# Spread products of the scales moved ahead of a slot's down products

## The chip, the cores and the metric

One core of one Trainium2 chip. The metric is the device time of one execution in microseconds (us), the median of the runs. TensorE multiplies (PE in rows; PEld is its loading of weights), VectorE is DVE, ScalarE is ACT, GpSimd is POOL, SyncE (SP) issues the transfers.

## The reference

Local and strided attention over 4 sequences of 576 tokens, 8 heads of 64, then two feed-forward layers over the 2304 tokens, all in float32:

```python
def _moe_ref(x, w_in, w_out) -> np.ndarray:
    h = x @ w_in
    g = h * np.cos(h)
    return (g @ w_out).astype(np.float32)
...
def _moe2_ref(x, w_gate, w_val, w_out) -> np.ndarray:
    g = x @ w_gate
    silu = g * (1.0 / (1.0 + np.exp(-g)))
    val = x @ w_val
    return (silu * val @ w_out).astype(np.float32)
```

The first layer is 512 to 2048 to 512 wide, the second 512 to 1536 to 512.

## The kernel before, in words

Every float32 factor is multiplied as two float16 parts, high and low, in three matmuls (`mm3`, L541 to L543). Before it is split, a matrix is multiplied by a power of two, its scale, so that its largest value fits. There are ten such scales for blocks of tokens and five for weights (w_in, w_out, w_gate, w_val, w_out2).

How a scale is made: VectorE takes the largest value per partition, column by column (L174 or L227 for weights, L521 for tokens). `spread_tops` takes the largest of the columns (L120), keeps its exponent (L123, L125 or L128) and multiplies an identity with it (L130): a diagonal of 128 values, `tops`. `common_scale` multiplies a matrix of ones with that diagonal on TensorE (L136, the spread product, 128x128 into a PSUM bank), so that all partitions hold all values, reads the largest (L137, `q`), and makes the scale and its inverse from it (L112 to L114).

The program is written out in the order of its engines. The tokens are in five blocks of 512, 512, 512, 384 and 384. In the first layer a slot is one block and one of 16 column tiles of w_in: `up1` is twelve matmuls (four contraction tiles times three) into a bank; `up1_a` to `up1_e` make the cosine product of them on ScalarE (L574, L581, L588), VectorE (L577, L584) and GpSimd (L589), spread over the next three slots; `up1_d` (L584) is the last to read the bank. `down_next` then multiplies the result of an older slot with w_out: twelve matmuls into four accumulators `acc0` to `acc3`, stored by L555 and L557 at a block's end. In the first HEAD = 14 slots there are no down products, and every second slot takes an accumulator's bank in place of one of its own (`spare`).

The main loop writes a slot in this order: the up products, the down products, `up1_a`, `up1_b` (L577), `finish`, one urgent piece (`pump_urgent`: splitting and scaling of the next block), half of the fill (`pump`: conversion and splitting of weights, their scans and scales), `up1_c`, `up1_d` (L584), the other half. A scale's steps are pieces of the fill or urgent pieces: one step makes the diagonal, a later one calls `common_scale`, which issues the spread product on TensorE behind all that the slot has there and reads it at once.

PSUM: four banks in a pool (`pm`), which the up products, the spread products and the products of the second layer take by turns through `bank()`; a tile takes the bank that was given free longest ago. The other four serve as accumulators.

Of the kernel before, what the change touches and what calls it, by code (L numbers as in the profile page):

```python
# [10 lines left out]
F32 = mybir.dt.float32  # L11
# [4 lines left out]
ALU = mybir.AluOpType  # L16
AX = mybir.AxisListType
# [14 lines left out]
LW = 64 + STRIDE  # L32
# [47 lines left out]
def build(tc, qk_l, qk_s, v_l, v_s, w_in, w_out, w_gate, w_val, w_out2, mask_l, mask_s, eye32, eye16, out):  # L80
    nc = tc.nc
    wide = w_in.dtype != F32
    with ExitStack() as ctx:
# [13 lines left out]
        ones16 = small.tile([128, 128], BF16, name="ones16")  # L97
# [5 lines left out]
        def col(name):  # L103
            count[0] += 1
            return small.tile([128, 1], F32, name=f"{name}{count[0]}")

        def brief(name):
            return small.tile([128, 1], F32, name=name, bufs=2)

        def finish_scale(p, bound):  # L110
            s, inv = col("s"), col("inv")
            nc.vector.reciprocal(out=s, in_=p)  # L112
            nc.vector.tensor_scalar(out=inv, in0=p, scalar1=2 / bound, scalar2=None, op0=ALU.mult)
            nc.vector.tensor_scalar(out=s, in0=s, scalar1=bound / 2, scalar2=None, op0=ALU.mult)  # L114
            return s, inv

        def spread_tops(parts, words):

            m, p = brief("m"), brief("p")
            nc.vector.tensor_reduce(out=m, in_=parts, op=ALU.max, axis=AX.X)  # L120
            if words:
                a = brief("a")
                nc.vector.tensor_scalar(out=a.bitcast(I32), in0=m.bitcast(I32), scalar1=3, scalar2=0x3F800000,  # L123
                                        op0=ALU.logical_shift_left, op1=ALU.bitwise_and)
                nc.vector.scalar_tensor_tensor(out=p.bitcast(I32), in0=m.bitcast(I32), scalar=0x40000000, in1=a.bitcast(I32),  # L125
                                               op0=ALU.bitwise_and, op1=ALU.bitwise_or)
            else:
                nc.vector.tensor_scalar(out=p.bitcast(I32), in0=m.bitcast(I32), scalar1=0x7F800000, scalar2=None, op0=ALU.bitwise_and)  # L128
            d = small.tile([128, 128], BF16, name="tops", bufs=2)
            nc.vector.tensor_scalar(out=d, in0=id16, scalar1=p, scalar2=None, op0=ALU.mult)  # L130
            return d

        def common_scale(d, bound):

            t, p = bank()[:, 0:128], brief("q")
            nc.tensor.matmul(out=t, lhsT=ones16, rhs=d, start=True, stop=True)  # L136
            nc.vector.tensor_reduce(out=p, in_=t, op=ALU.max, axis=AX.X)  # L137
            return finish_scale(p, bound)

        def prod(a, b, c=1.0, keep=True):  # L140
            r = col("c") if keep else brief("c")
# [6 lines left out]
        parts_w = {k: small.tile([128, a.shape[0] + 1], F32, name=f"pw_{k}") for k, a in MATS.items()}  # L148
# [30 lines left out]
        def later(cost, fn, key=None):  # L179
            fill.append((cost, fn, key))  # L180
# [3 lines left out]
        def step_fill():  # L184
            cost, fn, key = fill.popleft()
            fn()
            emitted.add(key)
            credit[0] -= cost

        def pump(share):  # L190

            credit[0] = min(credit[0] + share, max(share, 1.0))
            while fill and credit[0] > 0:
                step_fill()

        def need(key):
            while key not in emitted:
                step_fill()
# [53 lines left out]
        def begin(steps):  # L252

            if steps:
                later(*steps[0])
            while held:
                later(*held.popleft())
            held.extend(steps[1:])
# [24 lines left out]
        tops = {}  # L283

        def top_later(mat):
            begin([])
            later(0.6, lambda: tops.__setitem__(mat, spread_tops(parts_w[mat], wide)))

        def scale_later(mat, bound):
            later(0.6, lambda: scale_w.__setitem__(mat, common_scale(tops[mat], bound)))  # L290
# [81 lines left out]
        pm = ctx.enter_context(tc.tile_pool(name="pm", bufs=4, space=bass.MemoryType.PSUM))  # L372
# [26 lines left out]
        def load_v(i):  # L399
# [5 lines left out]
            else:  # L405
                v_t[i] = v_pair[i // 2 % 2]
                for u in range(2):
                    nc.sync.dma_start(out=v_t[i][64 * u:64 * u + SW, SP * u:SP * u + SP, :], in_=v_s[b, p % 2, u])

        def bank():  # L410
            return pm.tile([128, 512], F32, name="bank")

        def scale_q(i):
            q = qk_t[i][:, 0:S if is_local(units[i][1]) else QP]
# [100 lines left out]
        def scale_pieces(blk, scales):  # L515
            parts = small.tile([128, KC + 1], F32, name=f"parts{count[0]}_{blk}")
            count[0] += 1
            box = {}
            nc.gpsimd.memset(parts[:, KC:], TINY)
            for k in range(KC):  # L520
                yield 0.65, lambda k=k: nc.vector.tensor_reduce(out=parts[:, k:k + 1], in_=xy[blk][:, k, :], op=ALU.max, axis=AX.X,  # L521
                                                                apply_absolute_value=True)
            yield 0.6, lambda: box.__setitem__("top", spread_tops(parts, False))
            yield 0.6, lambda: scales.__setitem__(blk, common_scale(box["top"], TX))

        def split_pieces(blk, scales, dst):
            n = BLOCKS[blk][1]

            def piece(k):
                if k == 0:  # L530
                    dst[blk] = ring.tile([128, 2, 7, 512], F16, name="xs")
                t, s = dst[blk], scales[blk][0]
                if k < KC:
                    hi_part(t[:, 0, k, 0:n], xy[blk][:, k, :], s)
                if k:
                    lo_part(t[:, 1, k - 1, 0:n], xy[blk][:, k - 1, :], s, t[:, 0, k - 1, 0:n])
            for k in range(KC + 1):
                yield 0.7 if k else 0, lambda k=k: piece(k)
# [41 lines left out]
        def up1_c(c):  # L580
            nc.scalar.activation(out=c["w"], in_=c["w"], func=AF.Sin, scale=TWO_PI, bias=right)  # L581
# [188 lines left out]
        steps = deque()  # L770

        def keep_warm():
            t = bank()[:, 0:4 * LW].rearrange("p (n w) -> p n w", w=LW)
            nc.tensor.matmul(out=t, lhsT=id16, rhs=ml, start=True, stop=True)

        for k in range(len(gs) + LAGS[3] + 1):
            def group(lag):
                return gs[k - lag] if 0 <= k - lag < len(gs) else None
            i, g = 2 * (k // 6), k % 6
# [191 lines left out]
        def urge(pieces, key=None):  # L971
            urgent.extend((c, f, key) for c, f in pieces)
# [8 lines left out]
        def need_urgent(key):  # L981
            while key not in emitted or any(u[2] == key for u in urgent):
                pump_urgent()
# [24 lines left out]
        def load_w7(s):  # L1008
            if s < len(slots):
                need("pairs")  # L1010
                nc.sync.dma_start(out=w7_slots[s % W7S], in_=w7_d[slots[s][1]])

        for blk in range(NBLK):
            for m in range(M1):
                n = BLOCKS[blk][1]
                if slot < EARLY:
                    slot += 1
                    continue
                if blk == 0:
                    need(("in", m))  # L1020
                if m == 0:
                    if blk:
                        need_urgent(("xs", blk))
                    if blk == NBLK - 1:
                        urge(fold_pieces(0, sy, ys, spans), ("ys", 0))
                if m == (2 if blk else XM) and blk + 1 < NBLK:
                    urge(scale_pieces(blk + 1, sx))
                    urge(split_pieces(blk + 1, sx, xs), ("xs", blk + 1))
                c = up1(blk, m, spare=slot // 2 % KC if slot % 2 and slot < HEAD - 4 else None)
                if blk == NBLK - 1 and m in (7, 14):  # L1030
                    load_w7(m // 7 - 1)
                lag = 99 if slot < HEAD else max(MINLAG, HEAD - 2 - int((slot - HEAD) * RATE))
                work = 2.6 * n / 512
                while len(queue) + 1 > lag:
                    work += down_next()
                if slot >= HEAD:
                    open_weights(lag)
                up1_a(c)
                up1_b(steps[-1][2])
                if len(steps) > 2:  # L1040
                    finish(steps.popleft())
                budget = (work - 1.25 * n / 512) * (HSHARE if slot < HEAD else SHARE if blk < SB else SHARE2)
                pump_urgent()
                pump(budget * 0.5)
                up1_c(steps[-1][2])
                if len(steps) > 1:
                    up1_d(steps[-2][2])
                pump(budget * 0.5)
                steps.append((blk, m, c))
                slot += 1  # L1050
# [112 lines left out]
        for s, (blk, j) in enumerate(slots):  # L1163
            n = BLOCKS[blk][1]
            h = n // 2
            if s == 1:
                need(("out2", NPR - 1))
                for _ in range(RAW):
                    t = ring.tile([128, 512, 2] if wide else [128, 512], I32 if wide else F32, name="raw", bufs=RAW)
# [13 lines left out]
            w, x = w7_slots[s % W7S], ys[blk]  # L1183
# [139 lines left out]
```

## Time and profile before

| | |
|---|---|
| median of 3 runs | 900.7 us (898.19, 900.7, 902.98) |
| the profiled execution | 896.04 us, of which its span 894.3 |
| TensorE busy | 857.4 us, 96% |
| VectorE busy | 657.5 us, 74% |
| ScalarE busy | 521.7 us, 58% |
| mean granted TensorE clock | 0.984 |

A busy TensorE counts every matmul from its start to its end, and these overlap; its idle time is what is left. The attention ends at about 115 us, the first layer at about 515 us, the rest is the second layer. All fifteen spread products lie between 66 and 665 us.

### The profile page before, as it was taken

What the parts mean: (1) busy time and instruction counts of PE and PEld (TensorE: products, weight loads), DVE (VectorE), ACT (ScalarE), POOL (GpSimd) and SP (SyncE); (2) the same over time, 40 slices, a digit from 0 to 9 for tenths busy, and PEclk for the clock granted to TensorE, in tenths of its full rate; (3) what the DMA queues carried; (4) which work ended last, traced back from release to release, by engine and by line L of the source; (5) the groups of instructions that cost most, each with busy time, mean ns of one, the idle gap of its engine ahead of it and who ended that gap; (6) DMA issues with size and microseconds to landing.
All of it is one profiled execution on the core that took longest, in us unless ns stands there. A gap on an engine that the chain in (4) does not pass through costs nothing.

```text
span 894.3 us, 18463 instructions
## 1 busy us (share of the span) xinstructions
PE 857.4 (96%) x7228; PEld 607.3 (68%) x7228; DVE 657.5 (74%) x1287; ACT 521.7 (58%) x1046; POOL 198.7 (22%) x253
## 2 busy tenths in 40 slices
PE   7999999989999979899999998999999999999998
PEld 4677644434444434455655687888888899999998
DVE  4699899895758998969988368747765665665562
ACT  4789988763445668547888365545535434444440
POOL 3344324112134656422322200000000000000000
PEclk8699999999999989999999999999999999999999
DMA  9998842568545675661635435667777677888894
GB/s 293 345 319 252 268 150 68 166 191 270 195 142 192 214 234 184 220 208 49 218 124 207 165 142 199 261 207 262 245 235 270 223 264 283 308 284 320 310 331 155
DMA packets 53512, 200.61 MB, mean 224 GB/s; under 512 B 5456, under 2 KB 16208, under 8 KB 49584
## 3 DMA queue, kind: packets, MB, share of 16 engines
q1 hardware_dynamic: 53424, 199.42, 65.7%
q8 instruction: 57, 0.93, 0.4%
q14 instruction: 31, 0.25, 0.1%
HBM read 175.41 MB, written 23.99 MB: 223 GB/s over the span
## 4 chain that ended last, share of the span: by engine, by line
PE 73%; DVE 10%; ACT 6%; issue 6%; POOL 4%; DMA 1%; SPq 0%; ACTq 0%; POOLq 0%; DVEq 0%
PE acc L694 14%; PE bank L541 11%; PE bank L543 11%; PE bank L542 11%; PE acc L541 6%; PE acc L543 5%; PE acc L542 5%; PE bank L435 3%; PE po L488 3%; DVE arena L248 2%; POOL arena L916 2%; POOL arena L589 2%; ACT arena L245 2%; ACT arena L588 1%; PE tp L466 1%
## 5 line engine op out<-in xcount | busy, mean ns | idle before, releaser
L541 PE MATMUL bank<-xs,wi 128*128 128x256 f16 (+3 forms) x780 | 233.5, 299 | 20.3 <-DVE tb L584 9.9
L543 PE MATMUL bank<-xs,wi 128*128 128x256 f16 (+3 forms) x780 | 233.6, 300 | 0.0
L542 PE MATMUL bank<-xs,wi 128*128 128x256 f16 (+3 forms) x780 | 233.6, 299 | 0.0
L589 POOL TENSOR_TENSOR arena<-tb,arena 128x512 f16<-128x512 f32 (+1 forms) x80 | 91.6, 1146 | 241.7 <-ACT arena L588 219.0
L542 PEld LDWEIGHTS <-wi 128*128 128x128 f16 x880 | 86.2, 98 | 60.0 <-issue 27.6
L541 PE MATMUL acc<-arena 128*128 128x512 f16 (+1 forms) x320 | 114.7, 359 | 0.0
L542 PE MATMUL acc<-arena 128*128 128x512 f16 (+1 forms) x320 | 114.5, 358 | 0.0
L543 PE MATMUL acc<-arena 128*128 128x512 f16 (+1 forms) x320 | 114.5, 358 | 0.0
L541 PEld LDWEIGHTS <-wi 128*128 128x128 f16 x880 | 86.2, 98 | 38.2 <-issue 3.8
L543 PEld LDWEIGHTS <-wi 128*128 128x128 f16 x880 | 86.3, 98 | 35.4 <-issue 1.1
L694 PEld LDWEIGHTS <-arena 128*128 128x128 f16 x1080 | 100.7, 98 | 8.2
L679 POOL TENSOR_TENSOR wi<-tb 128x256 f32<-128x256 f32 (+1 forms) x30 | 20.2, 674 | 342.8 <-DVE tb L661 342.8
L661 DVE SCALAR_TENSOR_TENSOR tb<-tb,c,arena 128x512 f32<-128x512 f32 (+1 forms) x60 | 41.6, 693 | 62.8 <-ACT tb L656 62.6
L574 ACT ACTIVATE tb<-bank,quarter,c 128x512 int32<-128x512 f32 (+1 forms) x75 | 54.4, 725 | 50.0 <-PE bank L543 37.7
L542 PEld LDWEIGHTS <-arena 128*128 128x128 f16 x600 | 58.8, 98 | 34.2 <-issue 1.7
L694 PE MATMUL acc<-arena 128*128 128x256 f16 (+1 forms) x702 | 82.0, 265 | 0.0
L543 PEld LDWEIGHTS <-arena 128*128 128x128 f16 x600 | 58.7, 98 | 33.0 <-issue 0.3
L541 PEld LDWEIGHTS <-arena 128*128 128x128 f16 x600 | 58.7, 98 | 32.7 <-issue 0.3
L664 ACT ACTIVATE arena<-tb 128x256 f16<-128x256 f32 (+3 forms) x59 | 28.9, 489 | 79.9 <-DVE tb L661 79.9
L1191 DVE TENSOR_TENSOR arena<-bank,cv 128x512 f32<-128x512 f32 (+1 forms) x60 | 38.1, 635 | 44.9 <-PE bank L543 44.3
L588 ACT ACTIVATE arena<-tb 128x512 f16<-128x512 f32 (+1 forms) x80 | 46.5, 581 | 36.1 <-PE acc L543 32.7
L541 PE MATMUL bank<-xs,arena 128*128 128x256 f16 (+1 forms) x240 | 62.9, 262 | 1.2 <-DVE arena L1191 1.2
(147 smaller groups left out, 1716.9 us busy)
## 6 DMA issues: line engine op xcount, KB each, us to landing
wi<-w SPq DMA_DIRECT2D x20, 1792.0 KB
arena<-w SPq DMA_DIRECT2D x60, 576.0 KB, 5.2
raw<-w_out SPq DMA_DIRECT2D x56, 512.0 KB, 4.0
arena<-w SPq DMA_DIRECT2D x10, 1792.0 KB
raw<-w_gate SPq DMA_DIRECT2D x24, 512.0 KB, 4.6
raw<-w_val SPq DMA_DIRECT2D x24, 512.0 KB, 4.4
w<-arena SPq DMA_DIRECT2D x42, 256.0 KB, 2.0
raw<-w_in SPq DMA_DIRECT2D x16, 512.0 KB
```

What stands on the lines that cost most here:

```text
L435: nc.tensor.matmul(out=self.sc[r, i, :], lhsT=qk_t[self.i][r, q0:q0 + 64], rhs=qk_t[self.i][r, k0:k0 + w], start=i == 0, stop=False)
L488: nc.tensor.matmul(out=self.po[64 * h:64 * h + 64, i * qn:i * qn + qn], lhsT=v_t[self.i][0:r, t, 64 * h:64 * h + 64], rhs=pt[:, 64 * h:64 ...
L541: nc.tensor.matmul(out=o, lhsT=w[:, 0, c], rhs=x[0], start=first, stop=False, **kw)
L542: nc.tensor.matmul(out=o, lhsT=w[:, 0, c], rhs=x[1], start=False, stop=False, **kw)
L543: nc.tensor.matmul(out=o, lhsT=w[:, 1, c], rhs=x[0], start=False, stop=last, **kw)
L574: nc.scalar.activation(out=c["w"].bitcast(I32), in_=c["ph"], func=AF.Identity, scale=turn[c["blk"]], bias=quarter)
L588: nc.scalar.activation(out=g[:, 0, 0:n], in_=w, func=AF.Copy)
L589: nc.gpsimd.tensor_tensor(out=g[:, 1, 0:n], in0=w, in1=g[:, 0, 0:n], op=ALU.subtract)
L661: nc.vector.scalar_tensor_tensor(out=t, in0=t, scalar=s_g[c["blk"]], in1=c["C"][m][:, 1, 0:c["n"]], op0=ALU.mult, op1=ALU.mult)
L664: nc.scalar.activation(out=to, in_=src, func=AF.Copy, scale=2.0 ** -11)
L694: nc.tensor.matmul(out=o[:, c], lhsT=w[:, 256 * i + 128 * c:256 * i + 128 * c + 128], rhs=unit(u)[:, x:x + h], start=j == c == i == 0, sto ...
L1191: nc.vector.tensor_tensor(out=c["C"][m][:, :, h * right:h * right + h], in0=p, in1=t, op=ALU.add)
```

## The change

`common_scale` is taken apart. `ask` notes a diagonal as soon as it is made; `spread` issues the product; `largest` reads it. In the main loop of the first layer, the oldest noted diagonal is spread right behind the up products and ahead of the slot's down products, into `banks[0]`, which is the bank that the next slot's up products take; it is read at the latest after the first half of the fill. Where `common_scale` comes without a spread made before, it is made then, in a bank of its own. The pool of four tiles becomes four banks in fixed rotation, and a bank is given out only after what stands unread has been read.

```diff
-        def common_scale(d, bound):
-
-            t, p = bank()[:, 0:128], brief("q")
-            nc.tensor.matmul(out=t, lhsT=ones16, rhs=d, start=True, stop=True)
-            nc.vector.tensor_reduce(out=p, in_=t, op=ALU.max, axis=AX.X)
-            return finish_scale(p, bound)
+        spreads, unread = deque(), []
+
+        def ask(d):
+            box = dict(d=d)
+            spreads.append(box)
+            return box
+
+        def spread(box, t):
+            box["t"] = t[:, 0:128]
+            nc.tensor.matmul(out=box["t"], lhsT=ones16, rhs=box["d"], start=True, stop=True)
+            spreads.remove(box)
+            unread.append(box)
+
+        def largest(box):
+            if "p" not in box:
+                if "t" not in box:
+                    spread(box, bank())
+                box["p"] = col("q")
+                unread.remove(box)
+                nc.vector.tensor_reduce(out=box["p"], in_=box["t"], op=ALU.max, axis=AX.X)
+            return box["p"]
+
+        def common_scale(box, bound):
+            return finish_scale(largest(box), bound)
...
-            later(0.6, lambda: tops.__setitem__(mat, spread_tops(parts_w[mat], wide)))
+            later(0.6, lambda: tops.__setitem__(mat, ask(spread_tops(parts_w[mat], wide))))
...
+        banks = deque(pm.tile([128, 512], F32, name=f"bank{i}", bufs=1) for i in range(4))
+
         def bank():
-            return pm.tile([128, 512], F32, name="bank")
+            for box in list(unread):
+                largest(box)
+            banks.rotate(-1)
+            return banks[-1]
...
-            yield 0.6, lambda: box.__setitem__("top", spread_tops(parts, False))
+            yield 0.6, lambda: box.__setitem__("top", ask(spread_tops(parts, False)))
...
-            t = bank()[:, 0:4 * LW].rearrange("p (n w) -> p n w", w=LW)
+            t = banks[0][:, 0:4 * LW].rearrange("p (n w) -> p n w", w=LW)
...
                 c = up1(blk, m, spare=slot // 2 % KC if slot % 2 and slot < HEAD - 4 else None)
                 if blk == NBLK - 1 and m in (7, 14):
                     load_w7(m // 7 - 1)
+                asked = spreads[0] if spreads else None
+                if asked:
+                    spread(asked, banks[0])
...
                 pump(budget * 0.5)
+                if asked:
+                    largest(asked)
                 up1_c(steps[-1][2])
```

The order of the instructions shows what moves. On TensorE nine of the fifteen spread products stand earlier than before, by one to eleven groups of twelve matmuls; the other six, two of them in the attention and two in the second layer, stand where they stood. On VectorE only three readings move (those for w_out, w_gate and w_out2). On ScalarE, GpSimd and SP nothing moves. In the change's code the spread product is L142, its reading L152, the matmuls of `mm3` are L564 to L566, and L266 is the former L248, L578 the former L555, L600 the former L577, L607 the former L584, L544 the former L521.

TensorE, in the first fourteen slots, at the end of one slot's up products (`acc2`) and the start of the next's (`bank`, from w_in); before:

```order
L543 MATMUL acc2_2211<-xs_1239,wi_71 128x512
L541 LDWEIGHTS wi_71
L541 MATMUL bank_2237<-xs_1239,wi_71 128x512
L542 LDWEIGHTS wi_71
L542 MATMUL bank_2237<-xs_1239,wi_71 128x512
```

and with the change:

```order
L566 MATMUL acc2_2155<-xs_1211,wi_71 128x512
L142 LDWEIGHTS ones16_77
L142 MATMUL bank2_129<-tops_2151,ones16_77 128x128
L564 LDWEIGHTS wi_71
L564 MATMUL bank2_129<-xs_1211,wi_71 128x512
```

The spread product for w_out now stands two groups of twelve earlier, between the up products of two slots, and the second of them goes into the same bank.

TensorE, at the end of a slot and the start of the next at 254 us, where before the spread products for w_gate and w_val stood one behind the other:

```order
L543 MATMUL acc3_3123<-arena_2101 128x512
L136 LDWEIGHTS ones16_77
L136 MATMUL bank_3304<-tops_3051,ones16_77 128x128
L136 LDWEIGHTS ones16_77
L136 MATMUL bank_3313<-tops_3300,ones16_77 128x128
L541 LDWEIGHTS wi_71
L541 MATMUL bank_3325<-xs_2390,wi_71 128x512
```

and with the change, the same place:

```order
L566 MATMUL acc3_3047<-arena_2047 128x512
L142 LDWEIGHTS ones16_77
L142 MATMUL bank1_128<-tops_3221,ones16_77 128x128
L564 LDWEIGHTS wi_71
L564 MATMUL bank2_129<-xs_2328,wi_71 128x512
```

The product for w_val stays, in a bank of its own (bank1); the one for w_gate is gone from here. It stands eleven groups earlier, ahead of the last down products of block 0, and VectorE reads it (q23) in that slot, behind the stores of block 0 (`xy0`) and two more instructions; VectorE with the change:

```order
L578 TENSOR_SCALAR xy0_66<-acc1_2419,c16_2424 128x512
L578 TENSOR_SCALAR xy0_66<-acc3_2421,c16_2424 128x512
L600 SCALAR_TENSOR_TENSOR tb_2961<-bank3_130,c17_2462,tb_2961 128x512
L266 SCALAR_TENSOR_TENSOR xs_2924<-xy2_68,s20_2870,xs_2924 128x512
L152 TENSOR_REDUCE q23_3022<-bank1_128 128x1
L607 SCALAR_TENSOR_TENSOR tb_2919<-tb_2919,bank2_129 128x512
```

Before, VectorE had L584 right behind L248 at this place, and read that product 29 instructions later.

## Rows read from the trace of the kernel before

**Rows 1.** The waits: engine, tile and line, for whom; us in total, times, longest

```profile
ACT arena L588 <- PE acc L543: 32.7, 28, 3.6
...
DVE q L137 <- PE bank L136: 19.4, 7, 6.9
...
PE bank L541 <- DVE tb L584: 9.9, 8, 2.3
...
PE bank L541 <- DVE q L137: 6.6, 8, 3.0
```

**Rows 2.** TensorE's timeline at 210 us: start, us, instruction, idle time before it

```profile
209.75 0.22 PE L136 MATMUL bank<-tops,ones 128*128 128x128 bf16 x1
210.35 0.38 PE L541 MATMUL bank<-xs,wi 128*128 128x512 f16 x1 [0.38 <-DVE q L137]
```

**Rows 3.** TensorE's timeline in the first fourteen slots

```profile
127.10 0.38 PE L541 MATMUL bank<-xs,wi 128*128 128x512 f16 x1
...
140.11 0.22 PE L136 MATMUL bank<-tops,ones 128*128 128x128 bf16 x1
140.16 0.38 PE L541 MATMUL bank<-xs,wi 128*128 128x512 f16 x1
```

**Rows 4.** VectorE's timeline in the same slots

```profile
127.36 0.25 DVE L130 TENSOR_SCALAR tops<-id,p 128x128 bf16<-128x128 bf16 x1
...
128.19 0.68 DVE L521 TENSOR_REDUCE parts<-xy 128x1 f32<-128x512 f32 x1
...
140.38 0.28 DVE L137 TENSOR_REDUCE q<-bank 128x1 f32<-128x128 f32 x1
```

**Rows 5.** One line, L125: count, shortest/median/longest in ns, first and last start

```profile
L125 DVE SCALAR_TENSOR_TENSOR p<-m,a x5: 158/159/1132, 86.3 to 395.4; 128x1 int32<-128x1 int32 x5
```

**Rows 6.** TensorE's timeline at the last down products of block 0

```profile
225.89 0.38 PE L541 MATMUL acc<-arena 128*128 128x512 f16 x1
...
228.48 0.38 PE L541 MATMUL bank<-xs,wi 128*128 128x512 f16 x1
```

**Rows 7.** VectorE's timeline in that slot

```profile
230.01 0.74 DVE L248 SCALAR_TENSOR_TENSOR xs<-xy,s,xs 128x512 f16<-128x512 f32 x1
```

**Rows 8.** TensorE's timeline, the first up matmul of two later slots

```profile
260.16 0.38 PE L541 MATMUL bank<-xs,wi 128*128 128x512 f16 x1
...
267.93 0.38 PE L541 MATMUL bank<-xs,wi 128*128 128x512 f16 x1
```

**Rows 9.** VectorE's timeline, two readings L584 beside them

```profile
259.68 0.68 DVE L584 SCALAR_TENSOR_TENSOR tb<-tb,bank 128x512 f32<-128x512 f32 x1
...
269.42 0.68 DVE L584 SCALAR_TENSOR_TENSOR tb<-tb,bank 128x512 f32<-128x512 f32 x1
```

**Rows 10.** TensorE's timeline, the first down matmul of a slot of block 2

```profile
394.08 0.33 PE L541 MATMUL acc<-arena 128*128 128x384 f16 x1
```

**Rows 11.** VectorE's timeline beside it

```profile
395.61 0.26 DVE L130 TENSOR_SCALAR tops<-id,p 128x128 bf16<-128x128 bf16 x1
```

**Rows 12.** TensorE's timeline at 327 us: an up group's first matmul, the next group's first

```profile
327.18 0.58 PE L541 MATMUL bank<-xs,wi 128*128 128x512 f16 x1 [3.03 <-DVE q L137]
...
332.25 0.63 PE L541 MATMUL acc<-arena 128*128 128x512 f16 x1
```

**Rows 13.** VectorE's timeline ahead of it

```profile
323.21 0.67 DVE L584 SCALAR_TENSOR_TENSOR tb<-tb,bank 128x512 f32<-128x512 f32 x1
...
326.85 0.28 DVE L137 TENSOR_REDUCE q<-bank 128x1 f32<-128x128 f32 x1
```

**Rows 14.** Stretches: us, busy (instructions) of PE PEld DVE ACT POOL; granted clock; DMA share, GB/s

```profile
190.00:200.00 10.00, 8.49 (x39) 3.76 (x39) 9.55 (x17) 6.30 (x11) 2.32 (x2) 1.00 0.74 229
320.00:340.00 20.00, 14.33 (x54) 5.82 (x53) 17.81 (x28) 12.95 (x22) 11.36 (x13) 0.83 0.66 214
```

**Rows 15.** TensorE's timeline at 190 us

```profile
189.96 0.38 PE L541 MATMUL bank<-xs,wi 128*128 128x512 f16 x1 [2.33 <-DVE tb L584]
```

**Rows 16.** VectorE's timeline at 281 us

```profile
281.13 0.29 DVE L137 TENSOR_REDUCE q<-bank 128x1 f32<-128x128 f32 x1 [1.82 <-PE bank L136]
```

## The prediction

> **What bounds the kernel now.** I read the view of waits first, then the timelines of TensorE and VectorE around the fifteen spread products, then the stretches with their granted clock. A spread product is the product of a matrix of ones with the diagonal that L130 makes (L136); "q" is VectorE's reading of it (L137); an "up" product group is twelve matmuls of one slot into a bank, a "down" group the twelve that follow from older slots.
>
> In the waits [rows 1] see three things. TensorE's first up matmul of a slot waited 8 times, 6.6 us in all, for a q: the spread's bank is free only when q has read it, and the next slot takes that bank. VectorE waited 7 times, 19.4 us in all, for the spread product. And TensorE waited 9.9 us in all for L584, the last reader of an up group's bank. ScalarE in turn waited 28 times for the end of a down group (L588). So the engines hold each other: TensorE sets the time in most stretches, and VectorE does so where it is behind, as in the stretches of [rows 14], where TensorE is idle for 1.5 of 10 and 5.7 of 20 us while VectorE is busy for 9.55 and 17.81.
>
> **What the change takes away.** The usual wait for a q is the one at 210 us [rows 2]: the spread starts at 209.75, the next up matmul at 210.35, 0.60 later. Where nothing waits, the matmul behind a spread starts 0.05 later, at 140.11 and 140.16 [rows 3]. So a spread that sits at a slot's end costs 0.55, and one that sits ahead of a down group has those matmuls to cover its reading. The order shows nine spreads moved, and six of the eight waits for a q are of this short kind. One of the six lies in front of a stretch where TensorE then waits for VectorE anyway (281 us); I count it at nothing. Gain: 5 x 0.55 = 2.75 us.
>
> The two long waits for a q stay. At 327.18 TensorE waited 3.03 us [rows 12] because VectorE reached q only at 326.85 [rows 13]; the order on VectorE is unchanged there. The spread now stands ahead of the slot's down group and waits for the same L584, which ends at 323.88 [rows 13]; the down group follows it (2.59 us, as from 225.89 to 228.48 in [rows 6]), and the next up group starts behind the same q. Net nothing; the other long one likewise.
>
> **What it adds.** In its new place the spread has everything of the slot queued behind it on TensorE, in order, and the next up group is tied to its bank. Five places pay.
>
> 1. In the first fourteen slots there is no down group. The spread for w_out now stands right between two up groups and the second uses its bank. TensorE is there at 127.10 [rows 3]. The diagonal is ready at 127.36 + 0.25 = 127.61 [rows 4]; then VectorE has L577 and L521 to do, the latter until 128.19 + 0.68 = 128.87, then q, 0.28 as in the row at 140.38 [rows 4]: 129.15. The up matmul that would start at 127.15 starts at 129.19: 2.0 us. Of this about 1.0 hangs on L125, which here took its longest, 1.13 us, against 0.16 in its median [rows 5]; so 1.0 to 2.0, and I take 2.0, since the neighbours of that instruction don't change.
> 2. The next spread, at 140.11, doesn't move, but the group behind it now takes its bank. q ends at 140.38 + 0.28 = 140.66 [rows 4]; 140.70 instead of 140.16: 0.54.
> 3. The spread for w_gate comes one down group ahead of its reading only in appearance. Its slot is the last of a block: VectorE's queue there has the two stores of that down group, which wait for the group's end, then L577 and L248 until 230.01 + 0.74 = 230.75 [rows 7], and q behind them (the second order listing): 231.03. The next up group would start at 228.48 + 0.05 [rows 6]; it starts at 231.07: 2.54 us.
> 4. The spread for w_val is asked for and read in one slot. It takes a bank of the rotation for itself, so for the next slots each up group takes the bank of one slot later than before. The group at 260.16 [rows 8] then needs the L584 that ends at 259.68 + 0.68 = 260.36 [rows 9], 0.24 late; the one at 267.93 needs the L584 that ends at 269.42 + 0.68 = 270.10 and starts at 270.14: 2.21 late. These aren't added, the second holds the first.
> 5. The spread for w_out2 moves furthest, three groups of twelve. TensorE is at its new place at 394.08 [rows 10], before the diagonal is made at 395.61 + 0.26 = 395.87 [rows 11]; the whole down group behind it starts 1.83 late.
>
> Sum: 2.0 + 0.54 + 2.54 + 2.21 + 1.83 - 2.75 = **6.4 us longer**. The instructions themselves are the same in number and size, ScalarE's, POOL's and SP's orders are unchanged, so nothing else is added; a reading's own column in place of one of two shared ones takes no instruction. The sum is made on the profiled execution, 896.0 us, and gives 902.4 there. That execution lies 4.7 below the median of the runs shown, 900.7; I forecast on the median: **907.1 us**. A change of under 0.5%, some 4.5 us, is what a measurement of this kernel cannot tell from none.
>
> Of the clock the rows show this: after 2.33 us idle at 189.96 [rows 15] the stretch still has 1.00 granted; in the stretch 320 to 340 it is 0.83 [rows 14], and the up group from 327.18 to 332.25 [rows 12] took 5.07 us instead of 2.59, half the rate: the lower of the two levels, 1.2 GHz in place of 2.4. My new waits, 2.54 at the longest, are like the first, and the one around 320 is only rearranged, so I price the clock at nothing. [...]
>
> **The rivals.**
>
> *The new waits are absorbed by old ones.* TensorE waits for VectorE anyway at 189.96, 2.33 us [rows 15], and for the rest of the 9.9 us of L584 and the 3.03 of 327.18 [rows 1, 12]. If VectorE isn't held back when an up group is late, the 2.5 of the first two places vanish in the first wait and the 2.54 and 2.21 in those between 282 and 327. Then 1.83 - 2.75 = -0.9 is left: 899.8. For it: in [rows 14] VectorE is the busy engine. Against: VectorE's work on a slot starts with that slot's up group, by way of ScalarE, which also stands 32.7 us for down groups [rows 1]; a late group makes all three late. Chance 0.22.
>
> *VectorE gets ahead.* It stood idle 19.4 us for spreads, 1.82 of it at 281.13 [rows 16], just ahead of the stretch where TensorE waits for it most. If what it gains there stays with it up to 327, TensorE's wait there is 1.82 shorter, the clock may not fall behind it (5.07 - 2.59 = 2.5), and VectorE reads early enough that the five places cost nothing: -2.75 - 1.82 - 2.5 = -7.1, 893.6. It decides if q at the third place and the diagonal at the fifth are done before TensorE arrives. Against: those instructions stand behind stores that wait for TensorE, and at 281 VectorE's next work needs ScalarE, which waited for the same down group. Chance 0.08.
>
> *The clock falls with the new gaps.* At the third place, and at the longer single wait ahead of the down group near 320, half rate for one more group each costs 2 x 2.5 = 5: 912.1. For it: [rows 12]. Against: [rows 14, 15]. Chance 0.10.
>
> **How the numbers follow.** The forecast has 0.60: slower by 4.5 to 8, except for its lower edge (the first place at 1.0, the second and fourth partly absorbed), some 0.07 of it, which falls below 4.5 us. Slower by over 0.5%: 0.60 - 0.07 + 0.10 = 0.63. Within 0.5%: 0.22 + 0.07, less 0.02 for an absorbed case with all gains, = 0.27. Faster: 0.08 + 0.02 = 0.10. The range goes from the absorbed case, 899.5, to the clock's, 912; it leaves out the second rival and the edges. The forecast's own range is 904.5 to 909.
>
> **What would show it.** Right: the waits for q of 0.38 gone at 210, 387, 400 and 413; new waits of TensorE for q (some 1.4 us) near 129, for q (2.5) near 230, for the L584 of a slot (2) near 270, for the diagonal of L130 (1.9) near 400; the time to 327 longer by 5 to 7 us, and no further loss after 420. Wrong: if TensorE's idle time up to 330 doesn't grow, the waits were absorbed or VectorE got ahead; if the granted clock falls in a stretch other than that around 320, the third rival; if the loss lies after 520, something I haven't seen.

## The result, and the profile after

| | before | after |
|---|---|---|
| median of 20 runs each, us | 898.25 (894.29 to 908.64) | 903.34 (899.82 to 911.54) |
| ratio after to before | | 1.0061, 95% interval 1.004 to 1.0081 |
| span of the profiled execution, us | 894.3 | 898.0 |
| mean granted TensorE clock | 0.984 | 0.987 |
| TensorE busy, VectorE busy, us | 857.4, 657.5 | 854.8, 654.9 |

The change makes the kernel slower by 0.6%, 5.1 us between the medians. The busy times of TensorE and VectorE are slightly lower: the loss is waiting. The view of waits of the changed kernel (engine, tile and line, for whom; us in total, times, longest) answers to [rows 1]:

```profile
ACT arena L611 <- PE acc L566: 37.6, 31, 4.4
...
PE bank L564 <- DVE tb L607: 12.1, 9, 2.3
...
DVE q L152 <- PE bank L142: 11.0, 5, 6.6
...
PE bank L564 <- DVE q L152: 5.4, 4, 2.4
PE bank L142 <- DVE tb L607: 5.2, 1, 5.2
```

VectorE waits 8.4 us less for spread products, and TensorE waits for q 4 times instead of 8. That is what the change is meant to do, and it does it. But TensorE's waits for the last reader (now L607) have grown from 9.9 to 12.1, ScalarE's for down groups from 32.7 to 37.6, and three of the four waits for q are new, one of them long. Where they lie, TensorE's timeline shows (start, us, instruction, idle time before it):

```profile
126.65 0.22 PE L142 MATMUL bank<-tops,ones 128*128 128x128 bf16 x1 [0.40 <-DVE tops L130]
128.10 0.38 PE L564 MATMUL bank<-xs,wi 128*128 128x512 f16 x1 [1.23 <-DVE q L152]
...
141.65 0.38 PE L564 MATMUL bank<-xs,wi 128*128 128x512 f16 x1 [0.38 <-DVE q L152]
...
208.32 0.22 PE L142 MATMUL bank<-tops,ones 128*128 128x128 bf16 x1
208.38 0.38 PE L564 MATMUL acc<-arena 128*128 128x512 f16 x1
...
231.68 0.38 PE L564 MATMUL bank<-xs,wi 128*128 128x512 f16 x1 [2.36 <-DVE q L152]
...
263.61 0.38 PE L564 MATMUL bank<-xs,wi 128*128 128x512 f16 x1 [0.64 <-DVE tb L607]
...
273.12 0.38 PE L564 MATMUL bank<-xs,wi 128*128 128x512 f16 x1 [1.57 <-DVE tb L607]
...
292.87 0.38 PE L564 MATMUL bank<-xs,wi 128*128 128x512 f16 x1 [1.41 <-DVE tb L607]
...
328.63 0.26 PE L142 MATMUL bank<-tops,ones 128*128 128x128 bf16 x1 [5.22 <-DVE tb L607]
328.69 0.63 PE L564 MATMUL acc<-arena 128*128 128x512 f16 x1
...
398.89 0.22 PE L142 MATMUL bank<-tops,ones 128*128 128x128 bf16 x1 [1.68 <-DVE tops L130]
```

The spread at 208.32 answers to [rows 2]: the down matmul behind it starts 0.06 later and the wait for q is gone. The waits at 126.65, 128.10 and 141.65 stand in the head, where [rows 3] has none; 231.68 is the third place [rows 6], 263.61 and 273.12 the fourth [rows 8], 398.89 the fifth [rows 10], 328.63 the rearranged wait of [rows 12]; 292.87 is an old wait (1.35 in the kernel before).

To price each step I take the start of the same matmul in both TensorE timelines and subtract: the lag. At 120 us the executions already stand up to 11 us apart (the three of the change by 5.7); the two furthest behind, e1 and e7, show the lowest granted clock up to there, 0.82 and 0.86, against 0.89 to 0.96 in the others. So the lag is counted from 120 us on. The table gives by how much it grows in each stretch (times of the kernel before), for the change and for all experiments below. Each column is one execution against the one profile of the kernel before, so what chance did in that one is in every column: at 327 us e2, e3 and e4 show -0.61 to -1.27, though nothing moves there in them.

| stretch, us | after | e1 | e2 | e3 | e4 | e5 | e6 | e7 | e8 | e9 |
|---|---|---|---|---|---|---|---|---|---|---|
| 120 to 180, places 1 and 2 | 2.16 | 0.40 | 4.86 | -0.03 | 0.01 | 0.01 | 0.00 | 0.00 | 2.16 | 2.18 |
| 180 to 205 | 0.01 | 0.03 | 0.02 | 0.04 | 0.04 | 0.03 | 0.02 | 0.01 | 0.03 | 0.02 |
| 205 to 225, the wait at 210 | -0.54 | -0.54 | 0.00 | -0.54 | 0.00 | -0.54 | -0.55 | -0.54 | -0.54 | -0.54 |
| 225 to 245, place 3 | 2.57 | 4.26 | 0.00 | 0.06 | 4.26 | 0.06 | 0.06 | 0.06 | 2.57 | 4.26 |
| 245 to 256, the wait at 255 | -0.54 | -0.54 | 0.60 | -0.54 | -0.54 | -0.54 | -0.54 | -0.55 | -0.54 | -0.54 |
| 256 to 275, place 4 | 2.53 | 0.00 | 0.00 | -0.01 | 0.00 | 0.00 | 0.00 | 0.00 | 2.53 | 2.52 |
| 275 to 316, the wait at 281 | -0.48 | 1.44 | -0.01 | 0.01 | 0.00 | 0.00 | 0.00 | 0.02 | -0.49 | -0.48 |
| 316 to 360, the wait at 327 | -1.23 | -0.93 | -0.84 | -0.61 | -1.27 | -1.64 | -0.65 | -2.53 | -1.66 | -1.14 |
| 360 to 380 | 0.05 | 0.00 | 0.49 | 1.78 | 0.03 | 1.91 | 0.00 | 1.00 | -0.07 | 2.16 |
| 380 to 420, waits at 387, 400, 413, place 5 | 0.21 | 0.22 | 0.00 | -1.63 | 1.30 | -1.62 | -1.62 | -1.62 | 0.21 | 0.22 |
| 420 to the end | 0.06 | 0.09 | 0.04 | 0.03 | 0.03 | 0.02 | 0.02 | 0.02 | 0.06 | 0.06 |
| sum from 120 us | 4.80 | 4.43 | 5.17 | -1.44 | 3.85 | -2.31 | -3.26 | -4.13 | 4.26 | 8.72 |

### The profile page after: what moved, and what is told of

Read it like the earlier page. It is cut to its first block, busy times and chain, and to the rows that moved or that the text cites. A ratio compares the mean times of both kernels' runs of the same rounds, so it can differ in the third digit from the quotient of the medians.

```text
span 898.0 us, 18468 instructions
## 1 busy us (share of the span) xinstructions
PE 854.8 (95%) x7228; PEld 605.8 (67%) x7228; DVE 654.9 (73%) x1287; ACT 522.1 (58%) x1046; POOL 198.2 (22%) x253
## 4 chain that ended last, share of the span: by engine, by line
PE 73%; DVE 11%; issue 6%; ACT 4%; DMA 4%; POOL 3%; SPq 0%; ACTq 0%; DVEq 0%; POOLq 0%
PE acc L717 14%; PE bank L564 12%; PE bank L566 11%; PE bank L565 11%; PE acc L564 6%; PE acc L566 6%; PE acc L565 6%; PE bank L458 2%; PE po L511 2%; DVE arena L266 2%; DMA vl<-v_l 2%; POOL arena L939 1%; ACT arena L263 1%; DMA v_pair<-v_s 1%; DVE tb L600 1%
## 5 line engine op out<-in xcount | busy, mean ns | idle before, releaser
L564 PE MATMUL bank<-xs,wi 128*128 128x256 f16 (+3 forms) x780 | 232.6, 298 | 21.2 <-DVE tb L607 12.1
L566 PE MATMUL bank<-xs,wi 128*128 128x256 f16 (+3 forms) x780 | 232.6, 298 | 0.0
L564 PE MATMUL acc<-arena 128*128 128x512 f16 (+1 forms) x320 | 115.5, 361 | 0.0
L566 PE MATMUL acc<-arena 128*128 128x512 f16 (+1 forms) x320 | 115.3, 360 | 0.0
L564 PEld LDWEIGHTS <-wi 128*128 128x128 f16 x880 | 86.0, 98 | 35.7 <-issue 0.7
L566 PEld LDWEIGHTS <-wi 128*128 128x128 f16 x880 | 86.0, 98 | 34.8
L564 PEld LDWEIGHTS <-arena 128*128 128x128 f16 x600 | 58.9, 98 | 40.3 <-issue 8.2
L566 PEld LDWEIGHTS <-arena 128*128 128x128 f16 x600 | 58.9, 98 | 33.5 <-issue 1.1
L611 ACT ACTIVATE arena<-tb 128x512 f16<-128x512 f32 (+1 forms) x80 | 46.5, 581 | 39.2 <-PE acc L566 37.6
L564 PE MATMUL bank<-xs,arena 128*128 128x256 f16 (+1 forms) x240 | 62.9, 262 | 1.2 <-DVE arena L1219 1.2
```

What stands on the lines that cost most here:

```text
L564: nc.tensor.matmul(out=o, lhsT=w[:, 0, c], rhs=x[0], start=first, stop=False, **kw)
L566: nc.tensor.matmul(out=o, lhsT=w[:, 1, c], rhs=x[0], start=False, stop=last, **kw)
L611: nc.scalar.activation(out=g[:, 0, 0:n], in_=w, func=AF.Copy)
```

## The experiments

The theory at test is the forecast's: each spread product that moves saves 0.55 where its reading is prompt, and five places pay, each for its own reason. Its rivals were that old waits absorb the new ones, that VectorE gets ahead, and that the clock falls; after the result a further one stood beside them: that the fixed rotation costs, and the earlier product nothing.

**e1: the moved products without the rotation.**

```diff
-        banks = deque(pm.tile([128, 512], F32, name=f"bank{i}", bufs=1) for i in range(4))
-
         def bank():
-            for box in list(unread):
-                largest(box)
-            banks.rotate(-1)
-            return banks[-1]
+            return pm.tile([128, 512], F32, name="bank")
...
-            t = banks[0][:, 0:4 * LW].rearrange("p (n w) -> p n w", w=LW)
+            t = bank()[:, 0:4 * LW].rearrange("p (n w) -> p n w", w=LW)
...
-                    spread(asked, banks[0])
+                    spread(asked, bank())
```

> The change with its spread products moved as they are, but with the pool of four banks of the kernel before (a tile takes the bank given free longest ago) in place of the fixed rotation. My forecast's steps: at 127 us only the wait for the diagonal is left (ready at 127.61, TensorE there at 127.10: 0.5 instead of 2.0), nothing at 140, 2.5 at 229 for the reading behind the block's stores, nothing at 260 and 268 (no bank is taken out of turn), 1.8 at 394 for the diagonal; new: the spread at 275.70 in its moved place meets the reader L584 that in the kernel before starts at 276.92 and takes 0.68, so up to 1.9. Gains of 0.55 at five or six places. Sum 0.5 + 2.5 + 1.9 + 1.8 - 3.0 = 3.7 us over the kernel before, a ratio of 1.004. Rival, the rotation costs and the earlier product does not: 2.75 to 3.3 us faster than before, 0.997. Rival, new waits absorbed: -0.5 to +0.5 us.

Measured: 902.03 against 897.82 us, ratio 1.0055 (1.0018 to 1.0092); by the time alone this isn't told from the change's 1.0061. TensorE's timeline:

```profile
137.36 0.23 PE L143 MATMUL bank<-tops,ones 128*128 128x128 bf16 x1 [0.40 <-DVE tops L130]
137.42 0.38 PE L560 MATMUL bank<-xs,wi 128*128 128x512 f16 x1
...
290.94 0.22 PE L143 MATMUL bank<-tops,ones 128*128 128x128 bf16 x1 [1.78 <-DVE tb L603]
291.00 0.38 PE L560 MATMUL acc<-arena 128*128 128x512 f16 x1
```

(This execution runs 10 us behind the kernel before from the attention on, and 14 at the end.) The head costs 0.4, the wait for the diagonal alone; the 1.23 for q in the same bank is gone, and so is place 4. But a new wait of 1.78 comes with the spread of 281 us: ahead of the down group it needs a bank whose last reader, L603 here, isn't done (e3, which leaves that spread where it was, has no step there). So most of the rotation's 2.5 at place 4 isn't to be had back by giving up the rotation; VectorE's lateness in that stretch catches TensorE one spread later. Of the 4.43, 1.7 is matmuls at half rate (0.63 us each in place of 0.38, started 0.43 apart in place of 0.22) behind the third place's wait (e4 shows them). The other 2.7 are 2.1 below the 4.80 of the change's profile, which has none there. The rotation's share of the change is some 2.4: 1.8 in the head and 0.6 from 256 to 316; the 0.3 the other way at 327 is slow matmuls (2.4 us of them here, 2.1 in the change). The rotation is not the whole cause.

**e2: the rotation without the moves.**

```diff
-                    spread(box, bank())
+                    spread(box, banks[0])
...
-                asked = spreads[0] if spreads else None
+                asked = None
```

Every spread product then stands in the bank that the next slot takes; in the change only the moved ones do.

> The fixed rotation alone: every spread product stays where it stood before the change, in the bank that the next slot takes. My forecast's reading: the short waits for q stay; in the first fourteen slots the spread for w_out at 132.28 now sits in the bank of the group behind it, and its reading, which ends at 135.15 + 0.28 = 135.43 in the kernel before, holds that group from 132.34 to 135.47: 3.1 us; 0.54 at 140 as in the change; sum 3.7 over the kernel before, ratio 1.004, all of it before 141 us. Rival, the early product is all that costs: 0, ratio 1.000. Rival, absorbed: the 3.1 is gone by the wait of 2.33 us at 190 (rest 1.4 or less).

Measured: 900.85 against 897.82 us, ratio 1.0023 (0.9991 to 1.0055); by the time alone this isn't told from no change. The steps tell it: 4.86 before 180 us. TensorE's timeline in the head:

```profile
132.45 0.22 PE L142 MATMUL bank<-tops,ones 128*128 128x128 bf16 x1
135.64 0.58 PE L564 MATMUL bank<-xs,wi 128*128 128x512 f16 x1 [2.97 <-DVE q L152]
136.02 0.63 PE L565 MATMUL bank<-xs,wi 128*128 128x512 f16 x1
```

The wait is the expected one (3.1 of lag); what I had not expected is the 0.63 behind it in place of 0.38: some 7 matmuls at half rate, 1.5 us more. At 254 us the two spreads now wait for one another's reading, 0.60 more. In the head, then, the tie to the next slot's bank is what costs: 4.86 with the late product (1.5 of it the half rate), 2.16 with the early one, 0.40 with the early one and no tie.

**e3: only the moves that the theory calls free.** e1's kernel with a list of slots (e1 has them all):

```diff
+        AHEAD = (23, 28, 51, 54, 57)
...
-                asked = spreads[0] if spreads else None
+                asked = spreads[0] if spreads and slot in AHEAD else None
```

The spread for w_gate stands in slot 28 instead of 26, that for w_out2 in slot 54 instead of 53.

> Only those spread products are moved ahead of a slot's down products whose diagonal is there and whose reading has no late work ahead of it on VectorE: slots 23, 28, 51, 54 and 57, with the pool of the kernel before; the first fourteen slots, the spreads near 281 and 327 us and those of the second layer stay. My forecast's gain, 5 x 0.55 = 2.75 us, with no loss: lag of TensorE against the kernel before -0.55 at each of 210, 255, 388, 401 and 413; ratio 0.997. Rival, the time is set by VectorE and not by these waits: 0, ratio 1.000, each 0.55 is given back in the next wait for L584. Rival, VectorE gets ahead: over 4 us faster, 0.995.

Measured: 894.87 against 897.82 us, ratio 0.9954 (0.9922 to 0.9986): faster than the kernel before. All five steps are there, five times 0.54 to 0.55, and no other before 316 us. Two slots later w_gate's product costs nothing, one slot later w_out2's neither. TensorE's timeline at two other places:

```profile
190.54 0.38 PE L560 MATMUL bank<-xs,wi 128*128 128x512 f16 x1 [2.35 <-DVE tb L603]
...
191.63 0.63 PE L561 MATMUL bank<-xs,wi 128*128 128x512 f16 x1
...
372.84 0.48 PE L560 MATMUL bank<-xs,wi 128*128 128x384 f16 x1 [2.99 <-DVE tb L603]
```

At 190 the old wait of [rows 15] is this time followed by 8 matmuls at half rate, 1.7 us; the next wait for VectorE, 1.51 us in the kernel before, is gone in turn, so that the table shows 0.04. And at 373 the two waits of 0.70 and 1.63 of the kernel before are one of 2.99, with slow matmuls behind it: +1.78 in that profile. The gains were not given back at VectorE's next wait each. That the one wait of 2.99 gives part of them back isn't shown: e2 and e9, which had gained nothing by then, have it too, and e6, with the same moves and one more, has not. Of e2's, of 2.97, no slow matmul came:

```profile
378.67 0.32 PE L564 MATMUL bank<-xs,wi 128*128 128x384 f16 x1 [2.97 <-DVE tb L607]
378.83 0.32 PE L565 MATMUL bank<-xs,wi 128*128 128x384 f16 x1
```

**e4: only the two moves that the theory calls dear.** As e3, with AHEAD = (26, 53).

> Only the two spread products for w_gate (three slots after its diagonal is asked for the chance, in the slot with a block's last down products) and w_out2 (before its diagonal is made) are moved, with the pool of the kernel before. My forecast's steps: +2.54 at 229, +1.83 at 394, -0.55 at 401 and 0 to -0.55 at 255: 3.3 to 3.8 us over the kernel before, ratio 1.004. Rival, absorbed: the 2.54 is gone by 330, at the waits for L584 between 282 and 327, so the lag ahead of 380 us is 0 to 0.5 and the end 1.3 to 1.8. Rival, clock: a further group at half rate behind one of the two gaps, lag at 235 or 400 up by 2.5 more.

Measured: 902.42 against 897.82 us, ratio 1.0032 (0.9996 to 1.0067), by the time alone not told from no change; steps 4.26 at place 3 and 1.30 between 380 and 420, which is 1.89 at place 5 less the 0.60 between the spread and the up group at its old place. TensorE's timeline:

```profile
231.28 0.38 PE L560 MATMUL bank<-xs,wi 128*128 128x512 f16 x1 [2.36 <-DVE q L153]
...
232.53 0.63 PE L561 MATMUL bank<-xs,wi 128*128 128x512 f16 x1
...
398.62 0.22 PE L143 MATMUL bank<-tops,ones 128*128 128x128 bf16 x1 [1.68 <-DVE tops L130]
```

The wait of 2.36 at the third place is the change's own to the hundredth, but here 8 matmuls at half rate follow, 1.7 us; both are still in the lag at 316 us (3.76 from 120 us on, 0.54 being saved at 255). The stretch behind the wait shows the granted clock (columns as in [rows 14]), first in the change's profile:

```profile
231.00:236.00 5.00, 4.32 (x21) 1.96 (x21) 4.96 (x11) 2.29 (x5) 1.50 (x2) 1.00 0.44 153
```

and then in e4's, 0.59 in place of 1.00, most of it at the lower level of 1.2 GHz:

```profile
231.00:235.00 4.00, 3.72 (x10) 1.38 (x10) 3.96 (x10) 0.40 (x1) 1.03 (x1) 0.59 0.39 121
```

Absorption is out for this place, and the clock rival is in part right.

**e5: zero products in the wait at 327.** e3's kernel, ahead of slot 41's up products:

```diff
+        zero16 = small.tile([128, 128], F16, name="zero16")
+        nc.gpsimd.memset(zero16, 0.0)
...
+                if slot == 41:
+                    b0, m0 = queue[0][0:2]
+                    assert 0 < m0 < M1
+                    for i in range(12):
+                        nc.tensor.matmul(out=acc_t[1, b0][i % KC][:, 0:n], lhsT=zero16, rhs=xs[blk][:, 0, 0, 0:n], start=False, stop=False)
```

> The third experiment's kernel (five spread products moved) and, in the wait for q at 327 us, twelve products of a matrix of zeros into the open accumulators, which add nothing to them (12 x 0.22 = 2.6 us in a wait of 3.03). In the profiles so far this wait was followed by 6 to 13 matmuls at half rate, 0.21 us extra each, 1.3 to 2.8 us. If the clock there costs what it seems: no matmul at half rate near 327, 2 us faster than the third experiment, 4.7 faster than the kernel before, ratio 0.995. Rival, VectorE sets the time: the group starts earlier at full rate, but the next wait for L584, 1.63 us at 373 in the kernel before, grows by the same 2 us; ratio as in the third experiment, -2.7 us. Rival, the clock doesn't care for products of zeros: half rate as before.

Measured: 896.29 against 898.48 us, ratio 0.9967 (0.9933 to 1.0002), not told from no change, where 4.7 us were expected. TensorE's timeline:

```profile
325.86 0.22 PE L145 MATMUL bank<-tops,ones 128*128 128x128 bf16 x1 [2.66 <-DVE tb L605]
325.91 4.44 PE L1054 MATMUL acc<-xs,zero 128*128 128x512 f16 x12
330.19 0.38 PE L562 MATMUL bank<-xs,wi 128*128 128x512 f16 x1
```

The twelve took 4.44 instead of 2.6: 8 of them ran at half rate, and the up group behind them at the full one, 1.1 later than the 3.25 after the spread at which it started in e3. So the clock goes down already behind the 2.66 ahead of the spread, and I had put the filling into the wrong wait. The stretch gains 1.0 over e3, not 2. At 373 a single wait of 2.57 with slow matmuls behind it comes as in e3, +1.91.

**e6: the spread of the wait at 327 moved too.** As e3, with AHEAD = (23, 28, 40, 51, 54, 57).

> The third experiment's kernel with one more spread product moved, that of the wait at 327 us (slot 40). In the profile of the change this place gave 0.9 us where I had forecast nothing: one wait of 5.22 for L584 instead of 2.64 and 3.03, and 10 matmuls of the down group at half rate instead of 13 of the up group. Expected if that is its mechanism: TensorE's lag falls by 0.5 to 0.9 between 320 and 335, a wait of 5.2 before the spread, 10 or 11 matmuls at half rate; 3.2 to 3.6 us faster than the kernel before. Rival, it was chance of the clock: 0 from the waits (5.22 against 5.67 is in both), and the rest by the count of slow matmuls alone. Rival, VectorE sets the time: given back by 380 us.

Measured: 896.0 against 898.48 us, ratio 0.9953 (0.9926 to 0.9981). TensorE's timeline:

```profile
322.80 0.27 PE L143 MATMUL bank<-tops,ones 128*128 128x128 bf16 x1 [5.23 <-DVE tb L603]
322.86 0.63 PE L560 MATMUL acc<-arena 128*128 128x512 f16 x1
...
327.98 0.54 PE L560 MATMUL bank<-xs,wi 128*128 128x512 f16 x1
```

and VectorE's:

```profile
325.71 0.28 DVE L153 TENSOR_REDUCE q<-bank 128x1 f32<-128x128 f32 x1
```

One wait of 5.23 instead of 5.67 in two [rows 12], and 13 matmuls at half rate, as many as in the kernel before: the step of -0.65 is then the arrangement alone, without luck in their number. At half rate the down group lasts 5.1 us instead of 2.59, so that q is read before it ends and the up group at 327.98 doesn't wait for it. In the change it was 10 matmuls, and the other 3 x 0.21 explain its -1.23. No wait of 2.99 at 373 came in this profile.

**e7: as e6, with twenty zero products ahead of that spread.** The edit of e5 with `slot == 40` and `range(20)`, just ahead of `asked`.

> As the run before it, with twenty products of a matrix of zeros into the open accumulators ahead of the moved spread (20 x 0.22 = 4.3 us in a wait of 5.22). Expected if the clock costs there what it seems: no matmul at half rate between 320 and 340, 2.1 to 2.3 us (10 or 11 x 0.21) less than the run before it, 5.3 to 5.9 us faster than the kernel before, ratio 0.994. Rival, VectorE sets the time: the group's 2 us come back as a longer wait for L584 at 373. Rival, no effect of zeros on the clock: as the run before it.

Measured: 894.63 against 898.48 us, ratio 0.9961 (0.993 to 0.9992). TensorE's timeline:

```profile
326.41 4.48 PE L1057 MATMUL acc<-xs,zero 128*128 128x512 f16 x20
331.81 0.22 PE L145 MATMUL bank<-tops,ones 128*128 128x128 bf16 x1 [0.91 <-DVE tb L605]
331.86 0.38 PE L562 MATMUL acc<-arena 128*128 128x512 f16 x1
...
335.06 0.38 PE L562 MATMUL bank<-xs,wi 128*128 128x512 f16 x1 [0.44 <-DVE q L155]
...
368.22 0.38 PE L562 MATMUL bank<-xs,wi 128*128 128x512 f16 x1 [1.71 <-DVE tb L605]
```

No matmul at half rate is left there, in this one profile (8 to 13 in the five that have the wait of 5.22 unfilled), 1.9 us better than e6 in that stretch; and with the down group at full rate a wait for q is back, 0.44. Half of the 1.9 comes back: the wait at 361 is 1.71 instead of 0.70. By the medians e7 is 3.9 us faster than the kernel before, where 5.3 to 5.9 were expected. Of e3, e5, e6 and e7 no time tells one from another; e3, e6 and e7 are faster than the kernel before by their intervals, by 0.4 to 0.5%; with the change's 0.6% above it that is, worked out from the ratios, about 1% less than the change.

**e8 and e9: the change itself, twice more.**

> The change itself once more, unaltered, for its profile alone: the wait of 2.36 us at the third place was followed by no matmul at half rate in the change's own profile, by 8 of them (1.7 us) in two kernels with the same wait. If that is chance of the execution: 8 at half rate in one of two further profiles, the other steps of TensorE's lag (2.2 before 141 us, 2.6 at the third place, 2.5 between 256 and 275, 1.9 at the fifth) as in the first profile. If it hangs on the kernel (fixed rotation against pool): none in either.

> As the run before it, a third profile of the unaltered change. Same expectations; between the two of them, at least one with matmuls at half rate behind the wait of 2.36 us if it is chance of the execution, none if it hangs on the kernel. The old wait of 2.3 us at 190, which was followed by 8 at half rate in five of the nine profiles so far, should show the same mixture.

Measured: 904.98 and 904.28 us, one run each, beside 899.37. The steps repeat to 0.03 up to 205 us and at places 4 and 5; the third place is 2.57 in e8 and 4.26 in e9. In e9 the two waits at 361 and 373 are moreover a single one of 2.98 with slow matmuls behind it, as in e2, e3 and e5: +2.16. TensorE's timeline of e9:

```profile
232.24 0.38 PE L564 MATMUL bank<-xs,wi 128*128 128x512 f16 x1 [2.36 <-DVE q L152]
...
233.66 0.63 PE L566 MATMUL bank<-xs,wi 128*128 128x512 f16 x1
```

So the half rate behind that wait is a matter of the execution, not of the kernel: 1 of 3 profiles of the change, 3 of 5 with e1 and e4. The old wait at 190 shows it in 7 of 11, and there it is made up each time by the next wait for VectorE.

## Why the prediction was right, and where it was off

The forecast, slower by 6.4 us for five places against five saved waits, holds: the 5.1 us between the medians lie in its 4.5 to 8. The time itself lies 3.8 below the forecast and just under its own range, 904.5 to 909; of this 2.45 is the starting point (I used the median of three runs, 900.7; twenty give 898.25). That the 4.80 of the change's first profile comes so near the medians is in part luck: its other two give 4.26 and 8.72, nearly all of the difference between these being matmuls at half rate and the single wait at 373, which I hadn't priced.

*The gain* was 5 x 0.55 and is 5 x 0.54 (e3 shows the five alone). *Place 1*, 2.0: 2.01 by the lag, with the same 1.13 us of L125 [rows 5] in it, which that instruction takes in all eleven profiles. *Place 2*, 0.54: 0.54; then 0.3 comes back, where an old stall for L584 at 150.85 is gone. *Place 3*, 2.54: 2.57, and VectorE's timeline there is the one that the forecast read from the order:

```profile
228.06 0.75 DVE L578 TENSOR_SCALAR xy<-acc,c 128x512 f32<-128x512 f32 x1 [6.70 <-PE acc L566]
229.36 0.75 DVE L578 TENSOR_SCALAR xy<-acc,c 128x512 f32<-128x512 f32 x1 [0.55 <-PE acc L566]
230.02 0.74 DVE L600 SCALAR_TENSOR_TENSOR tb<-bank,c,tb 128x512 f32<-128x512 f32 x1
230.68 0.74 DVE L266 SCALAR_TENSOR_TENSOR xs<-xy,s,xs 128x512 f16<-128x512 f32 x1
231.34 0.28 DVE L152 TENSOR_REDUCE q<-bank 128x1 f32<-128x128 f32 x1
```

The two stores wait for the down group that stands behind the spread, and q stands behind them: the product was early, its reading was not. *Place 4*, 2.21 with the second wait holding the first: 2.53, as steps of 0.80 and 1.74 at the two waits of 0.64 and 1.57 (a matmul's 0.38 otherwise overlaps the next by 0.16, and a wait takes that away too). *Place 5*, 1.83: 1.90.

Three steps failed. First, "I count it at nothing", of the short wait at 281: it gave 0.54, since the waits for L607 behind it hardly grew (1.41 at 292.87, 1.35 before). Second, "Net nothing" at 327: -1.23. At full rate it comes near the truth, since the wait for q is then back (0.44 in e7); but the down group now runs at half rate and covers the reading of q, which is worth 0.65 (e6). The rest, 10 slow matmuls instead of 13, is luck: with the old arrangement e2, e3 and e4 have 7 to 11. The other long wait, near 460, did stay. These two are 1.8 of the sum; with the 0.3 that comes back behind place 2, place 4's 0.3 more than forecast, and small ones they take it from 6.4 to the 4.8 measured. Third, "I price the clock at nothing" for new waits that I took to be like that at 190: in one of three profiles of the change, and in e1 and e4, the same wait brought 1.7 us of half rate. The row at 190 that I argued from [rows 14, 15] was one execution, and in 7 of 11 that stretch looks otherwise. Over the eleven profiles half rate came behind the waits around 327 us in all but the filled one of e7 (a pair of 2.64 and 3.03, one of 5.22, or 2.66 in e5), behind three of the four single ones at 373 (2.57, 2.98 and 2.99, not 2.97), behind 10 of the 16 of 2.33 to 2.36 at 190 and at the third place, and behind those of 1.2 to 1.8 never. The Trainium skill (page "TensorE: Matmul & The Clock Gate", section "Why this matters for your kernels") names a length of idle between bursts of matmuls from which the lower rate comes back, and the 2.36 us of the third place stay below it; here the measurement differs, and no one length parts the cases.

The rivals: absorption is excluded for the five places, whose steps are in the lag at the end but for the 0.3 behind place 2; it is real for slow matmuls at 190 and for half of what e7 wins. VectorE getting ahead is excluded by e3's steps, which are the five short waits and no more; its time alone, ratio 0.9954, could not tell the two apart. The clock falling is partly true, as said, though not at the place that I named ahead of the down group near 320, where one half-rate group took the place of another.

Beside L125's 1.13 us GpSimd's timeline has this, in the change's profile as in the ten others:

```profile
125.14 1.16 POOL L612 TENSOR_TENSOR arena<-tb,arena 128x512 f16<-128x512 f32 x1 [1.41 <-ACT arena L611]
```

and VectorE's:

```profile
125.18 1.13 DVE L125 SCALAR_TENSOR_TENSOR p<-m,a 128x1 int32<-128x1 int32 x1
```

L125 starts 0.04 us after this GpSimd instruction and ends 0.015 behind its end, in all eleven. No run moves the one away from the other, so that GpSimd holds it up is argued from the times and not tested; the half of place 1 that hangs on L125 would then be a matter of when the two meet.

What stays open: what decides whether a wait of 2.35 us is followed by half rate, and why the waits at 361 and 373 are one in four of the eleven profiles.

## What to carry to other kernels

Moving a product earlier on an in-order engine pays only if its input is ready and its reading stands early on the reader's queue; before such a move, read what is ahead of the reading there, above all stores that wait for the very work the product was moved past. A buffer tied to the next step in a fixed order gives the reader's lateness to that step; choose the slots by these two conditions (e3) in place of one rule for all. And price the clock behind a wait from several executions, not from one.

## What the runs showed of the hardware

Waits of TensorE of the same length to 0.01 us are followed by full rate in one execution and by some 8 matmuls at half rate in another (2.36 us at the third place, e8 and e9). Products with a matrix of zeros kept the clock up in the one profile that shows it: behind twenty of them and a wait of 0.91 us the next group ran at full rate (e7), where 13 matmuls were slow without them (e6). And one VectorE instruction, the 128x1 of L125 near 126 us, takes 1.13 us in all eleven profiles, seven times its median, and ends each time 0.015 us behind a GpSimd instruction that had started 0.04 before it.
